# Batch 0's attention in plain float32, its probabilities turned on TensorE, and small work shared out anew over the engines

## The chip, the core and the metric

The kernel runs on one core of a Trainium2 chip. The metric is device time in microseconds (us) of one execution, as the median of three runs. The engines are TensorE (PE; PEld is its weight load), VectorE (DVE), ScalarE (ACT), GpSimd (POOL) and the DMA engines, whose transfers SyncE (SP) issues here.

## The reference

Block-causal attention (blocks of 64) is followed by a mixer over tokens and channels; 8 batches, 8 heads, 576 positions, head size 64, all in float32.

```python
scores = scale * np.matmul(q, k.transpose(0, 1, 3, 2))
scores = np.where(block_i >= block_j, scores, -1000000000.0)
attn = softmax(scores)
x = np.matmul(attn, v)                    # heads side by side: (8, 576, 512)
theta = x @ w_theta
y = einsum('ts,bsd->btd', w_tok_r, x * cos(theta)) + einsum('ts,bsd->btd', w_tok_i, x * sin(theta))
u = x + y
out = u + maximum(u @ w_ch, 0)
```

The weights w_theta, w_tok and w_ch arrive in float64, as pairs of 32-bit words.

## The kernel before

**Split products.** To keep float32's accuracy at the speed of narrow types, nearly every factor is split into a high and a low part, and a product is three matmuls: high x high, low x high, high x low. For q and k the parts are in a reduced-precision float32 type (F32R: `q_high`, `k_high` on POOL, L495 to L501; `q_low`, `k_low` on DVE, L503 to L510); for v, the probabilities, x, z and the weights in float16 (`v_first` on ACT, `v_second` on DVE, L515 to L520; `high` on ACT, `low` on DVE, L571 to L576). The profile prints F32R as f32 or fp32r.

**Attention.** A pair is two heads, whose scores lie in the upper and lower 64 rows of the array and run side by side. Per pair: loads of q, k and v; splits; `scores` "ab" (row blocks 3 and 2) and "c" (1 and 0) and `first_scores` "d"; nine `maxima` on DVE and nine `exponentials` on ACT, which write a head's probabilities `t`, 1664 columns wide; `high` and `low`, then `turn`, a DMA transpose of both parts from `p` to `pt` that SP issues (L578); `weighted` (L591, L596), the product with v, 42 matmuls of 65 columns for a head and 12 more for the second of a pair; `normalise` on DVE. Batch 0 has pairs 0 to 3.

**Mixer.** x is turned (batch 0 on TensorE, L650, from float32; later batches by DMA), split (`x_high`, `x_low`), multiplied by w_theta (`theta`, L680, 60 matmuls of 512 columns), turned into sines and cosines on ACT, whose function table changes between exponential and sine (L706, L563). `times_x` (L719, mostly POOL) multiplies them by x, `z_high` (ACT) and `z_low` (POOL or DVE) split them, `mix` (L743) multiplies by w_tok, `take_u` adds x, which `add_parts` and `unscale` (DVE, L751) prepared, `u_high` and `u_low` (POOL, L767; in the last batch DVE) split u, and `channel` (L775) multiplies by w_ch. In the first stage the 17 weight tiles also pass ACT and DVE (`exponent`, `narrow`, `most`, `high_part`, `low_part`); the largest size of a weight sets a power of two as its scale.

**Order.** Every step is a part with its needs. A number in the table TIMES for each part sorts them, and each engine's queue gets its instructions in that order and runs them strictly in it. BANKS says which of the eight PSUM banks a step takes. RUNNING inserts filler matmuls of ones at given places of the order (L955), whose result is not used; 111 in all.

Of the kernel before, what the change touches and what calls it, by code (L numbers as in the profile page):

```python
# [29 lines left out]
Z_POOL = (0, 1, 3)  # L30


TIMES = [
# [974 lines left out]
```

## Time and profile before

| what | value |
|---|---|
| time, median of 3 runs | 730.01 us (728.07 to 731.66) |
| profiled execution, its span | 725.2 us (no time beside the span is on its page) |
| mean granted TensorE clock | 0.971 |
| instructions | 18373 |
| HBM read, written | 43.06 MB, 9.44 MB |

The span runs from the first to the last instruction of one execution. The time of a run also has what lies around the span. Busy shares count an instruction's whole duration; matmuls overlap in the pipeline, so a busy TensorE says that something was under way. "Idle before, releaser" names what an engine waited for last.

### The profile page before, as it was taken

Reading aid. Unit: us, or ns where it says so; the run is one execution under the profiler, and the core shown is the slowest. Engines: PE = TensorE matmul, PEld = TensorE weight load, DVE = VectorE, ACT = ScalarE, POOL = GpSimd, SP = SyncE. Lnnn points to the kernel's source line nnn. Section 1 sums busy time; section 2 is a strip of 40 time slices with the busy share of each in tenths; the row PEclk is TensorE's granted clock in tenths of the full one; section 3 lists DMA queues with packets and bytes.
Section 4 is the critical chain, followed back from the end, with each engine's and each line's share of the span. In section 5 each row is a group of like instructions: output and inputs, shape, how many; then the busy total and the mean of one; then the engine's idle time right before and its main releaser. Section 6 shows DMA issues by size and latency. Waiting matters only on the chain.

```text
span 725.2 us, 18373 instructions
## 1 busy us (share of the span) xinstructions
PE 667.2 (92%) x7565; PEld 527.2 (73%) x7565; DVE 602.7 (83%) x1103; ACT 518.7 (72%) x813; POOL 295.1 (41%) x334
## 2 busy tenths in 40 slices
PE   8667497999979899999999999999999999999997
PEld 4455455789658776988688758877597868776777
DVE  5899998998988998899969977999889967963833
ACT  4978989665896869866986689866983879525410
POOL 3111128742283435833273525552273654342110
PEclk9768799999989999999999999999999999999999
DMA  8999944899979998679949948889967945570101
GB/s 290 256 257 238 266 101 102 172 184 188 238 137 168 175 204 179 156 166 203 209 132 171 183 114 155 203 164 195 208 125 163 189 96 113 109 127 5 66 1 66
DMA packets 272739, 117.38 MB, mean 162 GB/s; under 512 B 254096, under 2 KB 254096, under 8 KB 272656
## 3 DMA queue, kind: packets, MB, share of 16 engines
q1 hardware_dynamic: 272656, 116.22, 74.4%
q8 instruction: 59, 0.97, 0.6%
q14 instruction: 24, 0.20, 0.1%
HBM read 43.06 MB, written 9.44 MB: 72 GB/s over the span
## 4 chain that ended last, share of the span: by engine, by line
PE 48%; DVE 25%; DMA 12%; ACT 10%; issue 4%; POOL 0%; SPq 0%; DVEq 0%; ACTq 0%; POOLq 0%
PE ps L743 18%; PE ps L775 10%; PE ps L680 7%; PE ps L591 6%; DVE p L575 5%; DMA pt<-p 5%; PE ps L531 5%; DVE m L559 5%; ACT t L563 4%; DMA out<-u 2%; DVE v L519 2%; DVE zl L733 2%; DMA xt<-xp 1%; ACT p L572 1%; DMA raw_v<-in_v 1%
## 5 line engine op out<-in xcount | busy, mean ns | idle before, releaser
L563 ACT ACTIVATE t<-ps,m 128x576 f32<-128x576 f32 (+4 forms) x288 | 143.1, 556 | 65.4 <-DVE m L559 36.3
L743 PE MATMUL ps<-wT_h,zh 128*128 128x288 f16 x540 | 156.2, 289 | 9.6 <-ACT t L563 6.6
L743 PE MATMUL ps<-wT_h,zl 128*128 128x288 f16 x540 | 155.6, 288 | 0.6 <-DVE zl L733 0.4
L743 PE MATMUL ps<-wT_l,zh 128*128 128x288 f16 x540 | 155.6, 288 | 0.0
L559 DVE TENSOR_REDUCE m<-ps 128x1 f32<-128x448 f32 (+4 forms) x288 | 133.3, 508 | 11.1 <-PE ps L536 9.2
L575 DVE SCALAR_TENSOR_TENSOR p<-t,p 128x1664 f16<-128x1664 f32 x64 | 125.3, 1960 | 7.9 <-ACT p L572 7.8
L743 PEld LDWEIGHTS <-zh 128*128 128x128 f16 x1080 | 106.3, 98 | 28.5
L591 PE MATMUL ps<-v,pt 128*128 128x65 f16 x2688 | 95.9, 196 | 20.8 <-DVE xn L611 15.5
L572 ACT ACTIVATE p<-t 128x1664 f16<-128x1664 f32 x64 | 102.1, 1604 | 17.8 <-DMA pt<-p 17.6
L591 PEld LDWEIGHTS <-pt 128*128 128x128 f16 x2688 | 92.4, 99 | 28.0 <-DMA pt<-p 11.9
L680 PE MATMUL ps<-wth_h,xt 128*128 128x512 f16 x320 | 95.2, 379 | 2.6 <-DVE xt L668 0.9
L680 PEld LDWEIGHTS <-xt 128*128 128x128 f16 x480 | 46.3, 98 | 56.0 <-issue 3.4
L719 POOL TENSOR_TENSOR aa<-aa,xn 128x256 f32<-128x256 f32 (+1 forms) x84 | 64.3, 793 | 37.9 <-ACT aa L706 29.2
L775 PE MATMUL ps<-uh,wch_h 128*128 128x288 f32 x256 | 78.5, 307 | 0.4 <-DVE u L781 0.4
L531 PE MATMUL ps<-kh,qh 64*128 64x224 f32 (+3 forms) x384 | 66.3, 324 | 10.3 <-ACT t L563 9.2
L775 PE MATMUL ps<-ul,wch_h 128*128 128x288 f32 x256 | 75.5, 295 | 0.0
L775 PE MATMUL ps<-uh,wch_l 128*128 128x288 f32 x256 | 75.4, 295 | 0.0
L743 PEld LDWEIGHTS <-zl 128*128 128x128 f16 x540 | 53.3, 99 | 23.9 <-issue 10.8
L767 POOL TENSOR_TENSOR ul<-u,uh 128x576 fp32r<-128x576 f32 x28 | 44.1, 1576 | 63.3 <-ACT uh L761 63.1
L719 POOL TENSOR_TENSOR rr<-rr,xn 128x256 f32<-128x256 f32 x64 | 51.5, 829 | 40.9 <-ACT rr L707 35.4
L501 POOL TENSOR_SCALAR kh<-k 128x640 fp32r<-128x640 f32 x32 | 30.6, 957 | 73.8 <-DMA k<-in_kT 46.4
L680 PE MATMUL ps<-wth_l,xt 128*128 128x512 f16 x160 | 60.6, 379 | 0.0
(120 smaller groups left out, 1384.1 us busy)
## 6 DMA issues: line engine op xcount, KB each, us to landing
raw_v<-in_v SPq DMA_DIRECT2D x32, 384.0 KB, 4.2
q<-in_qT SPq DMA_DIRECT2D x32, 320.0 KB, 3.5
k<-in_kT SPq DMA_DIRECT2D x32, 320.0 KB, 3.5
out<-u SPq DMA_DIRECT2D x32, 288.0 KB, 2.6
w_raw<-in_w_tok SPq DMA_DIRECT2D x9, 576.0 KB, 5.5
...
pt<-p SPq DMA_TRANSPOSE x64, 6.4
```

Of the source, the lines that this page charges most:

```text
L501: nc.gpsimd.tensor_scalar(out=self.kh, in0=self.k, scalar1=1.0, scalar2=0.0, op0=ALU.mult, op1=ALU.add)
L531: nc.tensor.matmul(s[hh][:, col:col + n], lhsT=qq[rows, i * P:(i + 1) * P], rhs=kk[rows, k0:k0 + n], start=nn == 0 and (j == 0 or c == "ab ...
L559: nc.vector.tensor_reduce(out=m, in_=s, axis=AX.XY if i in (2, 3) else AX.X, op=ALU.max, negate=True)
L563: nc.scalar.activation(out=to, in_=s, func=AF.Exp, scale=1.0, bias=m)
L572: nc.scalar.mul(self.p[:, 0, :], self.t, LIFT)
L575: nc.vector.scalar_tensor_tensor(out=self.p[:, 1, :], in0=self.t, scalar=LIFT, in1=self.p[:, 0, :], op0=ALU.mult, op1=ALU.subtract)
L591: nc.tensor.matmul(o[:, i, :], lhsT=pp[:, block, :], rhs=vv[:, of, hh, :], start=nn == 0, stop=nn == n - 1)
L680: nc.tensor.matmul(g, lhsT=x[:, dt, part, i, :], rhs=ww[:, dt, :], start=(n == 0), stop=(n == 11))
L719: self.engine(n).tensor_tensor(out=cd, in0=cd, in1=self.rows(dt, i0, ni), op=ALU.mult)
L743: nc.tensor.matmul(g, lhsT=zz[:, kk, cols], rhs=ww[:, kk, ts], start=(n == 0 and kk == k0 and nn == 0), stop=(n == 4 and nn == 2))
L767: engine.tensor_tensor(out=ul[:, dt, ts], in0=self.u(dt)[:, ts], in1=uh[:, dt, ts].bitcast(F32), op=ALU.subtract)
L775: nc.tensor.matmul(g[:, 0:HS], lhsT=ww[:, dt, e * P:(e + 1) * P], rhs=uu[:, dt, th * HS:(th + 1) * HS], start=(n == 0), stop=(n == 11))
```

## The change

For batch 0 (pairs below `PLAIN`, 4) q, k, v and the probabilities stay whole in float32. Scores and the product with v are one float32 matmul where three stood: 13 for a pair's scores (39 before), 14 and 18 for its two heads' product with v (42 and 54). k is used as loaded, q and v get one scaling each. The probabilities are turned by 13 float32 transposes a head on TensorE into PSUM, in two halves of 8 and 5 blocks (`turn_half`, two banks each), and copied out with the factor LIFT by ACT or DVE (`keep_half`). So `high`, `low` and `turn`, and the remainders of q, k and v, are gone for these pairs. After them `count_keys` writes the columns of ones of v's tile anew for the later pairs.

A table ON names the engine (P, D or A) of single instructions: the splits `q_high` and `k_high`, the scaling of v, the copies, the products with x (`z`), the remainders `zl` and `ul`, and `unscale` (`xd`). Products with x on DVE go from 12 to 64 and on POOL from 148 to 96; `z_low` on DVE from 38 to 33; `u_low` on DVE from 8 to 18; 21 of 32 `unscale` go to ACT; of 60 splits of q and k that remain, with batch 0's four scalings of q, 28 are on ACT and 32 on POOL (64 on POOL before). Table loads of ACT go from 28 to 16, each time with one at the start. The whole order (PLACES in place of TIMES), the banks and the places of the fillers (56 in place of 111) are new.

```diff
...
-TIMES = [
-    100, 540, 615, 665, 745, 7122, 7220, 2640, 3104, 3223, 3533, 3619, 6960, 7153, 1595, 2055, 2169, 2280, 2497,
...
+PLACES = [
+    9, 39, 45, 50, 55, 274, 279, 7, 64, 66, 81, 86, 167, 174, 4, 20, 33, 37, 46, 150, 153, 12, 51, 57, 61, 62, 148,
...
-    (3, 0, 20), (33, 0, 26), (84, 0, 16), (137, 0, 8), (215, 0, 10), (265, 7, 10), (376, 0, 5), (442, 0, 12), (484,
-    0, 4)
+    (11, 0, 19), (35, 0, 10), (83, 0, 2), (96, 0, 5), (132, 5, 3), (443, 0, 8), (474, 3, 9)
 ]
+ON = {"qh": "APPPPPPPAAAAAAPPAPAAPAAPPAPAPAPA",
+      "vf": "DADP",
+      "cp": "DDADADAAADAAAAAA",
+      "kh": "DDDDPPPPAPPPPAAPAPPAAAPAPAAAPAPP",
+      "z": "DDDDPDDPPPPPPPPPDPPDPPPPPDDPPPDDPPDDDPDDPDPDPPPDDDPPPPPDPDPDPDPPPPPPDPDPPPPDDDPD",
+      "zl": "PPPDPPPPPDPPPPDPDPDPPPDDDPDPDPDDPDPPPPDDPPDDPDPPPPPDDDPPPPPDPPDPDDDPDDPDDDPPPDPD",
+      "xs": "DDDDDDDDDDDDDDDDDDDDDDDDDDDDDDDD",
+      "xd": "DAAADDAADADAAADAAAAAAAAADDDADAAD",
+      "ul": "PPPPPPPPDDPDPPPPDPDPDPDDPDPDDDDD"}
+PLAIN = 4
...
+    def engine_of(kind, n):
+
+        return {"P": nc.gpsimd, "D": nc.vector, "A": nc.scalar}[ON[kind][n]]
...
-            self.k = ld.tile([P, 640], F32, tag="kr", name="k")
+            self.k = ld.tile([P, 640], F32, tag="kr", name="k") if self.p >= PLAIN else \
+                ld.tile([P, 640], F32R, tag="kh", name="k", bufs=QK_BUFS).bitcast(F32)
             nc.sync.dma_start(out=self.k, in_=kT[self.b, self.pr])
+        def split(self, out, x, scale, engine):
+            if engine is nc.scalar:
+                engine.mul(out, x, scale)
+            else:
+                engine.tensor_scalar(out=out, in0=x, scalar1=scale, scalar2=0.0, op0=ALU.mult, op1=ALU.add)
...
-            nc.gpsimd.tensor_scalar(out=self.qh, in0=self.q, scalar1=QK_SCALE, scalar2=0.0, op0=ALU.mult, op1=ALU.add)
+            if self.p < PLAIN:
+                self.qh = self.qh.bitcast(F32)
+            self.split(self.qh, self.q, QK_SCALE, engine_of("qh", self.p))
...
-            nc.gpsimd.tensor_scalar(out=self.kh, in0=self.k, scalar1=1.0, scalar2=0.0, op0=ALU.mult, op1=ALU.add)
+            self.split(self.kh, self.k, 1.0, engine_of("kh", self.p))
...
+        def v_scaled(self):
+            x, engine = self.whole[:, :, :, 0:D], engine_of("vf", self.p)
+            if engine is nc.scalar:
+                engine.mul(x, self.v, self.batch.up)
+            else:
+                engine.tensor_scalar(out=x, in0=self.v, scalar1=self.batch.up, scalar2=1.0, op0=ALU.mult, op1=ALU.mult)
...
         def products(self):
+            if self.p < PLAIN:
+                return (self.qh, self.k),
             return (self.qh, self.kh), (self.ql, self.kh), (self.qh, self.kl)
...
+        def turn_half(self, half):
+            g = bank("tp", self.n, half)
+            for i in range((8, 5)[half]):
+                at_col = (8 * half + i) * P
+                nc.tensor.transpose(out=g[:, i * P:(i + 1) * P], in_=self.t[:, at_col:at_col + P], identity=ident)
+
+        def keep_half(self, half):
+            n = (8, 5)[half] * P
+            whole = self.turned.rearrange("p a c q -> p (a c q)").bitcast(F32)[:, 8 * half * P:8 * half * P + n]
+            engine, g = engine_of("cp", 2 * self.n + half), bank("tp", self.n, half)[:, 0:n]
+            if engine is nc.scalar:
+                engine.mul(whole, g, LIFT)
+            else:
+                engine.tensor_scalar(out=whole, in0=g, scalar1=LIFT, scalar2=None, op0=ALU.mult)
...
+            if pair.p < PLAIN:
+                products = [(self.turned.rearrange("p a c q -> p (a c q)").bitcast(F32).rearrange("p (c q) -> p c q", q=P), pair.whole)]
+            each = len(products)
...
-                self.engine(n).tensor_tensor(out=cd, in0=cd, in1=self.rows(dt, i0, ni), op=ALU.mult)
+                engine_of("z", (2 * self.b + hf) * 5 + n).tensor_tensor(out=cd, in0=cd, in1=self.rows(dt, i0, ni), op=ALU.mult)
...
-            engine = nc.gpsimd if n in Z_POOL and self.b < B - 1 else nc.vector
-            engine.tensor_tensor(out=zl, in0=cv, in1=zh, op=ALU.subtract)
+            engine_of("zl", (2 * self.b + hf) * 5 + n).tensor_tensor(out=zl, in0=cv, in1=zh, op=ALU.subtract)
...
-            nc.vector.tensor_scalar(out=self.u(dt), in0=self.u(dt), scalar1=self.batch.down, scalar2=None, op0=ALU.mult)
+            if engine_of("xd", self.b * NDT + dt) is nc.scalar:
+                nc.scalar.mul(self.u(dt), self.u(dt), self.batch.down)
+            else:
+                nc.vector.tensor_scalar(out=self.u(dt), in0=self.u(dt), scalar1=self.batch.down, scalar2=None, op0=ALU.mult)
...
-            engine = nc.vector if th else nc.gpsimd
-            engine.tensor_tensor(out=ul[:, dt, ts], in0=self.u(dt)[:, ts], in1=uh[:, dt, ts].bitcast(F32), op=ALU.subtract)
+            engine_of("ul", self.b * NDT + dt).tensor_tensor(out=ul[:, dt, ts], in0=self.u(dt)[:, ts], in1=uh[:, dt, ts].bitcast(F32), op=ALU.subtract)
...
+        split = [("ql", p), ("kl", p)] if p >= PLAIN else [("qh", p), ("k", p)]
+        add(("sab", p), step_of(pair.scores, "ab"), split, takes=[(("ab", p, hh), 2) for hh in range(2)])
...
+                free_pt = turn_of(f"pt{hh}", [("weighted", n)])
+                for half in range(2):
+                    needs = [key for key in made if (key[3] in (2, 3)) == (half == 0)]
+                    add(("tp", n, half), step_of(h.turn_half, half), needs, takes=[(("tp", n, half), 2)])
+                    add(("cp", n, half), step_of(h.keep_half, half), [("tp", n, half)] + free_pt, leaves=[("tp", n, half)])
+                turned_by = [("cp", n, half) for half in range(2)]
...
```

How the instructions move, at three places. The first is ACT's queue around the end of pair 0's exponentials; t_95 and t_96 before, t_91 and t_92 after are the two heads' probabilities. Before:

```order
L563 ACTIVATE t_95<-ps,m 128x192
L394 ACTIVATE w_val<-w_raw 128x512
L563 ACTIVATE t_96<-ps,m 128x192
L563 ACTIVATE t_96<-ps,m 128x448
L572 ACTIVATE p_100<-t_95 128x1664
L572 ACTIVATE p_101<-t_96 128x1664
L407 ACTIVATE wth_h,most_theta<-w_val 128x512
L407 ACTIVATE wT_h,most_tok<-w_val 128x576
```

and after the change:

```order
L571 ACTIVATE t_92<-ps,m 128x576
L571 ACTIVATE t_92<-ps,m 128x192
L396 ACTIVATE wth_h,most_theta<-w_val 128x512
L571 ACTIVATE t_92<-ps,m 128x448
L383 ACTIVATE w_val<-w_raw 128x512
L396 ACTIVATE wth_h,most_theta<-w_val 128x512
L590 ACTIVATE pt_99<-ps 128x1024
L396 ACTIVATE wth_h,most_theta<-w_val 128x512
```

The two whole-width high parts are gone; a copy of 1024 turned columns from PSUM stands between weight steps, and the copies of the first head's halves are on DVE.

The second is SP's queue in the first stage. Before:

```order
L513 DMA raw_v<-in_v 128x768
L385 DMA w_raw<-in_w_tok 128x1152
L385 DMA w_raw<-in_w_theta 128x1024
L579 DMA_TRANSPOSE pt_103<-p_101 128x26x128
L493 DMA k<-in_kT 128x640
L579 DMA_TRANSPOSE pt_102<-p_100 128x26x128
L385 DMA w_raw<-in_w_tok 128x1152 x2
L489 DMA q<-in_qT 128x640
L493 DMA k<-in_kT 128x640
L579 DMA_TRANSPOSE pt_102<-p_100 128x26x128
```

and after the change:

```order
L512 DMA raw_v<-in_v 128x768
L374 DMA w_raw<-in_w_theta 128x1024
L479 DMA q<-in_qT 128x640
L484 DMA k<-in_kT 128x640 x2
L374 DMA w_raw<-in_w_tok 128x1152 x2
L479 DMA q<-in_qT 128x640
L374 DMA w_raw<-in_w_tok 128x1152
L484 DMA k<-in_kT 128x640
L374 DMA w_raw<-in_w_tok 128x1152
L479 DMA q<-in_qT 128x640
L512 DMA raw_v<-in_v 128x768 x2
L374 DMA w_raw<-in_w_tok 128x1152 x2
```

The transposes from p to pt have left this stretch; only loads stand there, those of w_theta and v earlier.

The third is TensorE's queue around the first pair's product with v for its second head. Before (pt_103 holds the turned probabilities):

```order
L596 LDWEIGHTS pt_103
L596 MATMUL ps<-v_83,pt_103 64x65
L531 MATMUL ps<-kh,qh 128x288 x2
L531 MATMUL ps<-kh,ql 128x288 x2
L531 MATMUL ps<-kl,qh 128x288 x2
```

and after the change:

```order
L583 MATMUL ps<-ident_r,t_91 128x128 x5
L332 LDWEIGHTS ones
L332 MATMUL ps<-w_diag,ones 128x128
L617 MATMUL ps<-v_83,pt_99 128x65 x14
L622 MATMUL ps<-v_83,pt_99 64x65 x4
L539 MATMUL ps<-k,qh 128x288 x4
L539 MATMUL ps<-k,qh 128x224 x4
```

Where f16 products with a weight load each and sets of three score products stood, single float32 matmuls stand (18 for this head, 8 for the scores ab), and transposes of pair 1 (L583) are put ahead of the product.

## Rows read from the trace of the kernel before

**Rows 1.** The page, part 1: busy us, share of the span, instructions.

```profile
PE 667.2 (92%) x7565; PEld 527.2 (73%) x7565; DVE 602.7 (83%) x1103; ACT 518.7 (72%) x813; POOL 295.1 (41%) x334
```

**Rows 2.** The page, part 2: granted TensorE clock in 40 slices, tenths.

```profile
PEclk9768799999989999999999999999999999999999
```

**Rows 3.** Two stretches: length, busy us (instructions), granted clock, DMA share, GB/s.

```profile
0.00:97.20 97.20, 65.53 (x718) 47.76 (x719) 84.45 (x172) 76.43 (x138) 19.91 (x46) 0.82 0.92 245
97.20:726.00 628.80, 601.66 (x6847) 479.43 (x6846) 518.22 (x932) 442.23 (x676) 275.17 (x288) 0.99 0.72 149
```

**Rows 4.** Four shorter stretches, the same columns.

```profile
0.00:18.00 18.00, 15.21 (x89) 7.75 (x89) 10.06 (x18) 7.60 (x14) 5.69 (x27) 1.00 0.84 289
18.00:97.20 79.20, 50.31 (x630) 40.01 (x630) 74.40 (x155) 68.83 (x124) 14.22 (x19) 0.78 0.94 235
100.00:200.00 100.00, 93.90 (x1064) 71.96 (x1063) 90.43 (x155) 73.12 (x114) 47.60 (x45) 1.00 0.83 174
200.00:300.00 100.00, 92.22 (x1114) 72.83 (x1113) 87.97 (x157) 83.55 (x131) 52.81 (x61) 0.97 0.90 170
```

**Rows 5.** TensorE in order of time: start, us, what; matmuls' ends are modelled.

```profile
9.43 0.40 PE L531 MATMUL ps<-kh,qh 64*128 64x288 f32 x2
...
12.03 0.30 PE L543 MATMUL ps<-kh,qh 128*128 128x64 f32 x1
...
12.39 5.79 PE L955 MATMUL ps<-ones 128*128 128x512 bf16 x26
...
41.62 1.44 PE L591 MATMUL ps<-v,pt 128*128 128x65 f16 x42 [0.85 <-DMA pt<-p]
...
94.11 1.10 PE L650 MATMUL ps<-ident_r,xn 128*128 128x128 f32 x8
...
97.20 0.59 PE L680 MATMUL ps<-wth_h,xt 128*128 128x512 f16 x2 [0.92 <-DVE xt L668]
...
110.24 0.40 PE L531 MATMUL ps<-kh,qh 64*128 64x288 f32 x2
```

**Rows 6.** Groups by line, first 97.2 us: busy us, mean ns, idle before.

```profile
L575 DVE SCALAR_TENSOR_TENSOR p<-t,p 128x1664 f16<-128x1664 f32 x8 | 15.0, 1880 | 0.6 <-ACT p L572 0.6
L572 ACT ACTIVATE p<-t 128x1664 f16<-128x1664 f32 x8 | 12.7, 1606 | 1.2 <-DMA pt<-p 1.2
L563 ACT ACTIVATE t<-ps,m 128x576 f32<-128x576 f32 x10 | 7.5, 750 | 1.2 <-DVE m L559 1.1
L516 ACT ACTIVATE v<-raw_v,sizes 128x768 f16<-128x768 f32 x6 | 5.6, 957 | 1.3 <-PE ps L596 1.3
L519 DVE SCALAR_TENSOR_TENSOR v<-raw_v,sizes,v 128x768 f16<-128x768 f32 x5 | 5.1, 1011 | 0.0
L510 DVE TENSOR_TENSOR kl<-k,kh 128x640 fp32r<-128x640 f32 x6 | 4.9, 818 | 1.6 <-POOL kh L501 1.6
L505 DVE SCALAR_TENSOR_TENSOR ql<-q,qh 128x640 fp32r<-128x640 f32 x5 | 4.3, 857 | 3.8 <-POOL qh L497 3.8
```

**Rows 7.** DMA issues, first 97.2 us: median us from issue to landing.

```profile
pt<-p SPq DMA_TRANSPOSE x8, 7.1
```

**Rows 8.** Groups by line, whole run, as in rows 6.

```profile
L719 POOL TENSOR_TENSOR rr<-rr,xn 128x256 f32<-128x256 f32 x64 | 51.5, 829 | 40.9 <-ACT rr L707 35.4 <-DVE m L559 5.4
L751 DVE TENSOR_SCALAR u<-u,sizes 128x576 f32<-128x576 f32 x32 | 17.6, 561 | 0.0
L706 ACT ACT_TABLE_LOAD x14 | 18.0, 1283 | 0.2
L563 ACT ACT_TABLE_LOAD x13 | 16.7, 1283 | 1.2 <-DVE m L559 1.1
L719 DVE TENSOR_TENSOR aa<-aa,xn 128x256 f32<-128x256 f32 x8 | 2.9, 419 | 0.2 <-ACT aa L706 0.2
```

More of the change, by code (lines that the diff above doesn't have):

```diff
@@ L296, in attention_phase_mixer, with count_keys @@
     nc.gpsimd.memset(half_pi, math.pi / 2)
-    v_parts = [[const.tile([P, NV, 2, D + 1], F16, name=f"v{i}{j}") for j in range(2)] for i in range(2)]
-    for both in v_parts:
-        for part, x in zip(both, (1.0, 0.0)):
+    v_both = [const.tile([P, 2 * NV * 2 * (D + 1)], F16, name=f"v{i}") for i in range(2)]
+    v_parts = [[both.rearrange("p (a c h d) -> p a c h d", a=2, c=NV, h=2)[:, j] for j in range(2)] for both in v_both]
+    v_whole = [both.bitcast(F32).rearrange("p (c h d) -> p c h d", c=NV, h=2) for both in v_both]
+    def count_keys(*parts):
+        for part, x in zip(parts, (1.0, 0.0)):
             nc.gpsimd.memset(part[:, :, :, D:D + 1], x)
-    for both in v_parts:
-        nc.gpsimd.memset(both[0][0:64, 0, :, D:D + 1], 0.0)
-        nc.gpsimd.memset(both[0][64:P, 5, :, D:D + 1], 0.0)
+        nc.gpsimd.memset(parts[0][0:64, 0, :, D:D + 1], 0.0)
+        nc.gpsimd.memset(parts[0][64:P, 5, :, D:D + 1], 0.0)
+    for i in range(2):
+        count_keys(*([v_whole[i]] if i < PLAIN else v_parts[i]))
     t = [const.tile([P, WIDE], F32, name=f"t{i}") for i in range(2)]
@@ L484, in __init__ @@
             self.v1, self.v2 = v_parts[p % 2]
+            self.whole = v_whole[p % 2]
             self.v = raw_v[:, self.pr, :].rearrange("p (c h d) -> p c h d", c=NV, h=2)
@@ L531, in scores @@
                         nc.tensor.matmul(s[hh][:, col:col + n], lhsT=qq[rows, i * P:(i + 1) * P], rhs=kk[rows, k0:k0 + n],
-                                         start=nn == 0 and (j == 0 or c == "ab" and j == 1), stop=c == "ab" and j == 2 and nn == 2)
+                                         start=nn == 0 and (j == 0 or c == "ab" and j == 1), stop=c == "ab" and j == 2 and nn == len(self.products()) - 1)
             for hh in range(2):
@@ L542, in first_scores @@
             for nn, (qq, kk) in enumerate(self.products()):
-                nc.tensor.matmul(s[:, 0:64], lhsT=qq[:, 512:640], rhs=kk[:, 0:64], start=nn == 0, stop=nn == 2)
+                nc.tensor.matmul(s[:, 0:64], lhsT=qq[:, 512:640], rhs=kk[:, 0:64], start=nn == 0, stop=nn == len(self.products()) - 1)
         def where(self, hh, i):
@@ L596, in weighted @@
                             nc.tensor.matmul(o[rows, 4 + h, :], lhsT=pp[:, FIRST // P, h * 64:(h + 1) * 64], rhs=vv[:, 5, h, :],
-                                             start=nn == 0, stop=nn == 2)
+                                             start=nn == 0, stop=nn == each - 1)
         def normalise(self, step):
@@ L709, in attention_phase_mixer @@
         Z_PIECES = [(0, 0, 2, 0), (1, 0, 2, 4), (0, 2, 2, 2), (1, 2, 2, 6), (0, 4, 1, 8)]
-        def engine(self, n):
-            return nc.vector if self.b == B - 1 and n % 2 == 0 else nc.gpsimd
         def times_x(self, hf, n):
@@ L832, in attention_phase_mixer @@
             p = b * NPAIR + pr
-            add(("q", p), pairs[p].load_q, turn_of("qr", [("ql", p)]))
-            add(("k", p), pairs[p].load_k, turn_of("kr", [("kl", p)]))
-            add(("v", p), pairs[p].load_v, turn_of(f"raw_v{pr}", [("v2", p)]))
+            s_last = [("s" + c, p) for c in ("ab", "c", "d")]
+            add(("q", p), pairs[p].load_q, turn_of("qr", [("ql" if p >= PLAIN else "qh", p)]))
+            add(("k", p), pairs[p].load_k, turn_of("kr", [("kl", p)]) if p >= PLAIN else turn_of("kh", s_last, QK_BUFS))
+            add(("v", p), pairs[p].load_v, turn_of(f"raw_v{pr}", [("v2" if p >= PLAIN else "vf", p)]))
             add(("vz", p), step_of(batch.sum_of, pr), [("v", p)])
@@ L852, in attention_phase_mixer @@
         for c, first, second in (("q", pair.q_high, pair.q_low), ("k", pair.k_high, pair.k_low)):
-            add((c + "h", p), first, [(c, p)] + turn_of(c + "h", s_last, QK_BUFS))
-            add((c + "l", p), second, [(c + "h", p)] + turn_of(c + "l", s_last, QK_BUFS))
+            if p >= PLAIN or c == "q":
+                add((c + "h", p), first, [(c, p)] + turn_of(c + "h", s_last, QK_BUFS))
+            if p >= PLAIN:
+                add((c + "l", p), second, [(c + "h", p)] + turn_of(c + "l", s_last, QK_BUFS))
         free = turn_of(f"v{p % 2}", [("weighted", n) for n in heads])
-        add(("v1", p), pair.v_first, [("v", p), ("vc", b, 2)] + free)
-        add(("v2", p), pair.v_second, [("v1", p)])
-        add(("sab", p), step_of(pair.scores, "ab"), [("ql", p), ("kl", p)], takes=[(("ab", p, hh), 2) for hh in range(2)])
-        add(("sc", p), step_of(pair.scores, "c"), [("ql", p), ("kl", p)], takes=[(("c", p, hh), 1) for hh in range(2)])
-        add(("sd", p), pair.first_scores, [("ql", p), ("kl", p)], takes=[(("d", p), 1)])
+        if p < PLAIN:
+            add(("vf", p), pair.v_scaled, [("v", p), ("vc", b, 2)] + free)
+            if p >= PLAIN - 2:
+                add(("vo", p % 2), step_of(count_keys, *v_parts[p % 2]), turn_of(f"v{p % 2}", [("vo", p % 2)]))
+        else:
+            add(("v1", p), pair.v_first, [("v", p), ("vc", b, 2)] + free)
+            add(("v2", p), pair.v_second, [("v1", p)])
+        split = [("ql", p), ("kl", p)] if p >= PLAIN else [("qh", p), ("k", p)]
+        add(("sab", p), step_of(pair.scores, "ab"), split, takes=[(("ab", p, hh), 2) for hh in range(2)])
+        add(("sc", p), step_of(pair.scores, "c"), split, takes=[(("c", p, hh), 1) for hh in range(2)])
+        add(("sd", p), pair.first_scores, split, takes=[(("d", p), 1)])
         rows = [(hh, i) for i in (3, 2, 1, 0) for hh in range(2)] + [(1, 4)]
@@ L865, in attention_phase_mixer @@
             add(("m", p, hh, i), step_of(pair.maxima, hh, i), needs + (free if (hh, i) == (0, 3) else [("m", p, 0, 3)]))
-        free = [turn_of(f"t{hh}", [("low", n)]) for hh, n in enumerate(heads)]
+        free = [turn_of(f"t{hh}", [("low", n)] if p >= PLAIN else [("tp", n, half) for half in range(2)]) for hh, n in enumerate(heads)]
         for hh, i in rows:
@@ L876, in attention_phase_mixer @@
             h = Head(n, pair, hh, mixers[b])
-            add(("high", n), h.high, [("e", p, h_, i) for h_, i in rows if h_ == hh] + turn_of(f"p{hh}", [("turn", n)]))
-            add(("low", n), h.low, [("high", n)])
-            add(("turn", n), h.turn, [("low", n)] + turn_of(f"pt{hh}", [("weighted", n)]))
-            add(("weighted", n), h.weighted, [("turn", n), ("v2", p)] + turn_of("o", [("normalise", n, 2)]))
+            made = [("e", p, h_, i) for h_, i in rows if h_ == hh]
+            if p < PLAIN:
+                free_pt = turn_of(f"pt{hh}", [("weighted", n)])
[4 more added lines that the diff above has]
+                turned_by = [("cp", n, half) for half in range(2)]
+            else:
+                add(("high", n), h.high, made + turn_of(f"p{hh}", [("turn", n)]))
+                add(("low", n), h.low, [("high", n)])
+                add(("turn", n), h.turn, [("low", n)] + turn_of(f"pt{hh}", [("weighted", n)]))
+                turned_by = [("turn", n)]
+            add(("weighted", n), h.weighted, turned_by + [("v2" if p >= PLAIN else "vf", p)] + turn_of("o", [("normalise", n, 2)]))
             needs = [("weighted", n)] + turn_of("r", [("normalise", n, 2)], 2)
```

9 lines of the change are left out of this document (4 added, 5 removed), and 341 rows, old and new, of tables (BANKS, PLACES, TIMES).

## Prediction

> **What bounds the kernel now.** I read the shares of the engines first, then the same by stretches, then TensorE's instructions in order of time, and last the groups by line for prices.
>
> TensorE (PE) is busy for 667.2 of 725.2 us, VectorE (DVE) for 602.7, ScalarE (ACT) for 518.7 [rows 1]. That average hides two stages. The granted clock is below full speed in the first eighth of the span and nearly nowhere else [rows 2]. Batch 0's first product with w_theta is issued at 97.20 us [rows 5]; I call this T0 and cut there. Behind it lie 628.0 us of the span, with PE busy for 601.7 of them at a clock of 0.99 [rows 3]: the mixer and the other batches' attention are PE's. Ahead of it PE has 65.5 us of 97.2 at a clock of 0.82, and a good part of that is the filler products of L955. The reader should see who is full there: from 18 to 97.2 us DVE is busy for 74.4 of 79.2 us (94%), ACT for 68.8 (87%), and the DMA engines for 94% [rows 4]. So the first stage is DVE's, with ACT and the DMA close behind, and PE waits. The time is T0, plus 628.0, plus what lies around the span. The profiled span is 725.2 and the median of the three runs 730.0, so I add 4.8 at the end.
>
> **The change, stage one: DVE.** Batch 0 loses eight remainders of probabilities, 15.0 us ahead of T0. It also loses the remainders of q, k and v of its four pairs; some of batch 1's were already ahead of T0 and stay, so by the new order the count there falls by two of q (0.86 each), four of k (0.82) and three of v (1.01), 8.0 us [rows 6]. It gains five copies out of PSUM: one of 1024 columns, four of 640. No row has that operation; the nearest is ACT's exponential from PSUM, 0.75 us for 576 columns [rows 6], so 1024 columns lie between 0.75 and 1.33 (in proportion). I take 1.1, and 0.8 for 640, since nearly the same width is in the row: 4.3 us. Two scalings of v at about a v part's 0.95 add 1.9. DVE's 84.5 us ahead of T0 become 84.5 - 15.0 - 8.0 + 4.3 + 1.9 = 67.7.
>
> **ACT.** It loses eight high parts of probabilities (12.7 us) and four of v (3.7) [rows 6]. It gains eleven copies (seven of 1024 columns and four of 640: 10.9), one scaling of q (0.8) and one of v (0.9); by the new order one more high part, two more exponentials and one more sum stand ahead of T0 (3.5 together). 76.4 - 16.4 + 10.9 + 0.8 + 0.9 + 3.5 = 76.1 us: nothing gained. **ACT is the new bound of the stage.** It was idle for 10.4 of the first 18 us [rows 4]. The scores now need only k as it is loaded, second in SP's queue in place of fourth, and one scaling of q, no remainders; I give that 4 us, so 76 + 6 = 82 us if ACT never waits afterwards.
>
> **DMA.** Eight transposes leave SP's queue ahead of T0, each 7.1 us from issue to landing [rows 7]. What is left are the loads of weights, q, k and v, which kept pace at the start (289 GB/s in the first 18 us [rows 4]). I cost that stage's DMA at nothing: it lies beside ACT's 82 us.
>
> **PE, stage one.** Here stand the unknown prices.
> - Scores: a pair takes 2.96 us with three reduced-precision products (9.43 to 12.39) [rows 5]. The three leave out low times low; a whole float32 product could cost as little as one of them or as much as four. Between 0.99 and 3.95 a pair I take the upper end, 15.8 us for four pairs: with 192 to 320 moving columns nothing is left beside which a part could hide.
> - Transposes: 104. Eight float32 ones of L650 took 1.10 us [rows 5], 0.14 each: 14.3 us.
> - Products with v: 42 f16 products took 1.44 us, 0.034 each; the reduced-precision product with 64 moving columns, which also reads 32-bit weights, comes every 0.12 us [rows 5]. 112 full and 16 half products count as 120. The ends are one such product and, as above, four: 0.12 and 0.48. I take two, 0.24, nearer to the row: the stationary operand has two halves to load, and 65 moving columns, 0.034 us in f16, fit beside a load. 28.8 us; the ends are 14.4 and 57.6.
> - The rest: pair 4's scores 2.96, two thirds of pair 5's 2.0, 20 transposes of x 2.8, and 39 fillers at 13.04/60 = 0.22 each (the w_theta products have the same 512 columns [rows 5]) 8.5.
>
> Sum 15.8 + 14.3 + 28.8 + 16.3 = 75.2, from about 5 us on: 80. PE comes out just below ACT. Two in-order queues that feed each other at such loads don't run without waits: ACT's copy of a turned head stands in its queue behind the transposes, PE's next product behind the copy, the next pair's exponentials behind both. I add 6 us: **T0 = 88**. PE's waits should then be short, and its clock near full before T0.
>
> The trace shows no product of plain float32. The Trainium skill's page "FP8 and Floating Point Precision", section "TensorE Precision Notes", says that a true FP32 product takes four passes through the array. By that rule, with 0.12 us for a pass, an estimate for the products with v is 57.6 us in place of 28.8; that is the first rival below.
>
> **Stage two.** 628.0 us remain, less the 2.0 us of pair 5's scores done earlier. PE's list is otherwise the same, so the edits matter only where PE waits: 628.8 - 601.7 = 27 us [rows 3], of which 100 - 93.9 and 100 - 92.2 lie between 100 and 300 [rows 4]. The shared-out work: 52 more products with x on DVE (0.36 each against POOL's 0.83 [rows 8]), ten more remainders of u there (0.82, as k's [rows 6]), 21 scalings of u from DVE (0.56 [rows 8]) to ACT, 28 splits of q and k from POOL to ACT, and 27 table loads on ACT, 1.28 each [rows 8], become 15. DVE: 18.7 + 8.2 - 11.8 = +15, 518 to 533 of 628 us. ACT: 49 x 0.75 (576 columns [rows 6]) = 36.8, less 15.4, +21, 442 to 463. POOL gets less to do. I cost all of this at nothing: it lies beside PE's 96%; were that cover gone, DVE's 15 us or ACT's 21 would show, whichever queue PE then waited for. The relieved DVE should enter batch 1 with less backlog, and POOL's slow products leave the way from sines to mixing, so I take back 4 of the 14 us lost between 100 and 300; the bounds are 0 and 14.
>
> **Sum:** 88 + 628.0 - 2.0 - 4 + 4.8 = **714.8, say 715 us**.
>
> **Rivals.**
> 1. *Slower: the float32 products make PE the bound of stage one.* At 0.48 us each the sum of PE is 104 us, T0 = 109, nothing is taken back: 109 + 628.0 - 2.0 + 4.8 = 740. It decides from the price at which T0 exceeds 99 (99 + 630.8 = 730): 5 + 46.4 + 120w = 99, w = 0.40 us. For: no row has the operation, and the transposes and 64-column products suggest that loading 32-bit weights sets the pace. Against: the fillers that are left ahead of T0 stand at its beginning, so there is slack in PE there. Chance 0.20.
> 2. *Same: the removed load is not what T0 waits for.* ACT's 76 us stay; it now waits for PE's transposes where it waited for remainders, T0 stays near 97, and DVE's extra 15 us behind T0 eat what POOL's relief gives: 97 + 628.0 - 2.0 + 4.8 = 728. For: ACT's sum does not fall at all. Against: ACT had 20.8 us idle ahead of T0 [rows 3], and DVE was the fuller. Chance 0.13.
> 3. *More: both queues run dense and stage two loses nothing in batch 1.* T0 = 82, 14 us taken back: 82 + 628.0 - 2.0 - 14 + 4.8 = 699. For: the freed DVE and DMA. Against: PE's queue is in order and full as well. Chance 0.17.
>
> **The numbers.** My forecast (705 to 724) has 0.50, with rivals of 0.20, 0.13 and 0.17. About 0.5% is what a measurement of this kernel can tell from no change: 726.4 to 733.7. Faster 0.67, same 0.13, slower 0.20. For the range I leave out about half of rival 3 and half of rival 1: 700 to 738.
>
> **What would show it.** Right: the first w_theta product near 88 us; ahead of it DVE busy for about 68 us and ACT for about 76 with few idle stretches; a clock above 0.9 between 18 us and T0; the float32 products with v every 0.24 us; PE busy for 96% or more of the rest. Wrong: products with v at 0.40 us or more and ACT waiting for PE before its copies (rival 1); T0 near 97 with PE waiting for ACT (rival 2); or a stretch behind T0 in which PE waits for DVE's products with x, which would break the cost of nothing in stage two.

## The result and the profile after

The changed kernel takes 704.28 us (median of 4 runs, 702.33 to 706.13) where the kernel before takes 729.04 beside it (726.32 to 731.66): a ratio of 0.9664, 95% interval 0.9631 to 0.9696. The profiled execution took 702.33 us, with a span of 700.0.

First the page of the changed kernel, its shares and its clock (against [rows 1, 2]):

```profile
PE 671.2 (96%) x7434; PEld 538.9 (77%) x7434; DVE 598.7 (86%) x1126; ACT 532.6 (76%) x850; POOL 223.3 (32%) x252
...
PEclk9999999999999999999999999999999999999999
```

TensorE's clock no longer drops in the first eighth of the span. Then its first product with w_theta (T0) and, ahead of it, the float32 work of batch 0, in TensorE's order of time (start, duration):

```profile
9.64 2.00 PE L539 MATMUL ps<-k,qh 64*128 64x288 f32 x16
...
13.11 1.25 PE L998 MATMUL ps<-ones 128*128 128x512 bf16 x5
...
28.40 3.24 PE L617 MATMUL ps<-v,pt 128*128 128x65 f32 x28
31.47 1.04 PE L583 MATMUL ps<-ident_r,t 128*128 128x128 f32 x8
...
83.57 0.59 PE L706 MATMUL ps<-wth_h,xt 128*128 128x512 f16 x2 [0.65 <-DVE xt L694]
```

T0 is 83.57 us, against 97.20 [rows 5]. The span split there, and in stretches (busy us of PE, PEld, DVE, ACT, POOL, then clock, DMA share, GB/s), against [rows 3, 4]:

```profile
0.00:83.57 83.57, 73.46 (x612) 59.54 (x613) 68.67 (x162) 71.69 (x141) 21.29 (x49) 1.00 0.61 212
0.00:18.00 18.00, 14.26 (x73) 7.54 (x74) 6.47 (x14) 8.83 (x17) 2.70 (x21) 1.00 0.87 317
18.00:83.57 65.57, 59.20 (x540) 52.00 (x541) 62.20 (x149) 62.86 (x125) 18.59 (x28) 1.00 0.54 183
83.57:700.00 616.43, 597.74 (x6822) 479.37 (x6821) 530.04 (x965) 460.94 (x710) 202.06 (x203) 0.99 0.73 151
100.00:200.00 100.00, 92.85 (x1141) 74.98 (x1138) 92.56 (x172) 82.82 (x128) 39.17 (x41) 0.97 0.82 170
200.00:300.00 100.00, 97.92 (x1200) 79.97 (x1199) 92.45 (x162) 81.52 (x127) 36.65 (x38) 1.00 0.92 182
```

The span lost 25.2 us: 13.6 ahead of T0 and 11.6 behind it. From 18 us to T0 three engines are now full together (ACT 62.86 of 65.57 us, DVE 62.20, PE 59.20). Behind T0, DVE and ACT got busier by 11.8 and 18.7 us, and PE's time without work fell from 26.3 (628.0 - 601.7 [rows 3]) to 18.7; its busy time fell by the other 3.9.

### The profile page after: what moved, and what is told of

Same layout as the page of the kernel before. It is cut to its first block, busy times and chain, and to the rows that moved or that the text cites. A ratio compares the mean times of both kernels' runs of the same rounds, so it can differ in the third digit from the quotient of the medians.

```text
span 700.0 us, 18036 instructions
## 1 busy us (share of the span) xinstructions
PE 671.2 (96%) x7434; PEld 538.9 (77%) x7434; DVE 598.7 (86%) x1126; ACT 532.6 (76%) x850; POOL 223.3 (32%) x252
## 4 chain that ended last, share of the span: by engine, by line
PE 56%; ACT 16%; DVE 13%; DMA 9%; issue 3%; SPq 2%; POOL 0%; ACTq 0%; DVEq 0%; POOLq 0%
PE ps L765 24%; PE ps L799 9%; PE ps L617 7%; PE ps L539 6%; PE ps L706 6%; DMA pt<-p 3%; ACT t L571 3%; DVE m L567 3%; DMA raw_v<-in_v 3%; ACT p L595 2%; DMA q<-in_qT 1%; PE ps L998 1%; DMA xt<-xp 1%; ACT aa L732 1%; ACT aa L714 1%
## 5 line engine op out<-in xcount | busy, mean ns | idle before, releaser
L571 ACT ACTIVATE t<-ps,m 128x448 f32<-128x448 f32 (+4 forms) x288 | 143.9, 549 | 50.6 <-DVE m L567 34.6
L567 DVE TENSOR_REDUCE m<-ps 128x1 f32<-128x576 f32 (+4 forms) x288 | 134.7, 508 | 14.3 <-PE ps L544 14.0
L598 DVE SCALAR_TENSOR_TENSOR p<-t,p 128x1664 f16<-128x1664 f32 x56 | 106.4, 1902 | 9.7 <-ACT p L595 9.7
L617 PE MATMUL ps<-v,pt 128*128 128x65 f16 (+1 forms) x2576 | 108.2, 201 | 5.6 <-DMA pt<-p 2.2
L595 ACT ACTIVATE p<-t 128x1664 f16<-128x1664 f32 x56 | 88.7, 1590 | 8.9 <-DMA pt<-p 7.7
L617 PEld LDWEIGHTS <-pt 128*128 128x128 f16 x2352 | 78.5, 98 | 10.6 <-DMA pt<-p 4.8
L742 POOL TENSOR_TENSOR aa<-aa,xn 128x256 f32<-128x256 f32 (+1 forms) x60 | 45.8, 788 | 94.4 <-ACT aa L733 47.6
L765 PEld LDWEIGHTS <-zl 128*128 128x128 f16 x540 | 53.0, 98 | 18.7 <-POOL rr L742 4.1
L539 PE MATMUL ps<-kh,qh 64*128 64x288 f32 (+1 forms) x336 | 54.0, 313 | 1.5 <-ACT t L571 1.0
L799 PEld LDWEIGHTS ps<-uh,wch_h 128*128 128x128 f32 x256 | 48.1, 188 | 2.8 <-DVE rr L719 1.3
L539 PE MATMUL ps<-kh,ql 64*128 64x288 f32 (+1 forms) x336 | 48.9, 284 | 0.0
```

The costliest lines, as they stand in the source:

```text
L539: nc.tensor.matmul(s[hh][:, col:col + n], lhsT=qq[rows, i * P:(i + 1) * P], rhs=kk[rows, k0:k0 + n], start=nn == 0 and (j == 0 or c == "ab ...
L567: nc.vector.tensor_reduce(out=m, in_=s, axis=AX.XY if i in (2, 3) else AX.X, op=ALU.max, negate=True)
L571: nc.scalar.activation(out=to, in_=s, func=AF.Exp, scale=1.0, bias=m)
L595: nc.scalar.mul(self.p[:, 0, :], self.t, LIFT)
L598: nc.vector.scalar_tensor_tensor(out=self.p[:, 1, :], in0=self.t, scalar=LIFT, in1=self.p[:, 0, :], op0=ALU.mult, op1=ALU.subtract)
L617: nc.tensor.matmul(o[:, i, :], lhsT=pp[:, block, :], rhs=vv[:, of, hh, :], start=nn == 0, stop=nn == n - 1)
```

## The experiments

Twelve kernels ran, each timed in several rounds beside the kernel before; their ratios are to it, where the changed kernel has 0.9664. T0 (the "first channel product" of the expectations) and what follows it come from one profiled execution of each.

**1 to 3: one half of the change at a time.** They needed a rule that chooses banks, since the table of banks fits one order only; run 1 is the control for that rule.

```
e1: -at_bank = next(banks)
    +the banks that have been free longest; a step that finds none lets later steps go first
e2: e1, and PLACES, RUNNING, ON of the kernel before; turn_half and keep_half where "high" stood
e3: e1, and -PLAIN = 4
            +PLAIN = 0
    the splits of batch 0 beside the steps that had replaced them, its products with v one head later
```

> The changed kernel's steps in its own order and on its own engines, but every bank of PSUM chosen by a simple rule (the free bank that has been free longest) instead of the table of banks. It is the control for the two runs beside it, which need such a rule. My theory, that the banks themselves carry nothing: 702 to 708 us. Rival, that the chosen banks remove the waits of TensorE behind the first channel product: 708 to 716 us.

> Batch 0's attention in float32, transposed on TensorE, but the steps stand in the order of the kernel before and the engine table is the old one (banks by the rule of the control). Theory (float32 attention shortens stage one by freeing VectorE, the new order and sharing shorten the rest): the first channel product comes at 84 to 88 us instead of 97.2, what follows stays at 626 to 629 us, 712 to 718 us in all. Rival, the gain is the new order's alone: first channel product at 95 to 99 us, 725 to 730 us. Rival, the gain is float32's alone: 702 to 707 us.

> The new order and the new sharing over engines, but batch 0's attention in halves of float16 as before, its probabilities transposed by DMA. Theory: the first channel product at 95 to 98 us, what follows at 616 to 620 us, 712 to 718 us. Rival, the gain is the new order's alone: 702 to 707 us. Rival, float32's alone: 725 to 730 us.

Measured: e1 719.32 us, ratio 0.988 (0.9842 to 0.9917); e2 781.43, 1.0733; e3 768.67, 1.0569, with T0 at 86.12, 147.18 and 126.02 us. The control already missed: it loses 15 us. ScalarE, GpSimd and SyncE keep their orders in it, but on TensorE the scores of two pairs found no free bank and came later, at one place behind 24 mixing products and 42 products with v, at the other behind 12 and 54. One stretch shows the price, in e1 (columns as above):

```profile
150.00:170.00 20.00, 15.59 (x195) 13.63 (x192) 11.28 (x32) 8.57 (x15) 4.43 (x6) 0.74 0.65 132
```

and in the changed kernel:

```profile
150.00:170.00 20.00, 19.02 (x219) 17.88 (x216) 18.84 (x40) 14.78 (x23) 4.04 (x5) 1.00 0.82 167
```

In e1 TensorE, VectorE and ScalarE all have less to do there, and TensorE's granted clock is 0.74 in place of 1.00. In e2 and e3 the steps without a place in the table stood where I had put them, and both are far slower than either parent. So they don't say which half carries the gain; they say that neither half may be judged with steps put in by rule of thumb. The next runs leave an order as it is and change one thing in it.

**4 and 13: the sharing over engines.**

```
e4, changed kernel:
-ON = {"qh": "APPPPPPPAAAAAAPP...", "kh": "DDDDPPPPAPPP...", "z": "DDDDPDDPPPPPPPPP...", ...}
+ON = {"qh": "APPP" + "P" * 28, "kh": "P" * 32, "z": "P" * 70 + "DPDPD" * 2, "zl": "PPDPD" * 14 + "D" * 10,
+      "xd": "D" * 32, "ul": "P" * 28 + "D" * 4, ...}
e13, kernel before:
-self.engine(n).tensor_tensor(out=cd, ...)
+engine_of("z", (2 * self.b + hf) * 5 + n).tensor_tensor(out=cd, ...)
...
```

> The changed kernel with the old table of engines for the splits, the products with x and the sums (GpSimd carries the splits of w_channel's work and most z products again); order, banks and float32 attention as in the changed kernel. Theory, the order gives back the waits behind the first channel product and the sharing little of it: 704 to 708 us, first channel product at 83 to 85 us. Rival, the sharing carries them: 712 to 718 us, with TensorE waiting behind the first channel product for GpSimd.

> The kernel before, in its own order and with its own banks and attention, with the changed kernel's table of engines for the splits of q and k from batch 1 on, the products with x, the low halves of z and u, and the scaling of u. Theory after the run with the old table in the new order (table and order were made for each other): the first channel product stays at 96 to 98 us, what follows does not gain, 626 to 645 us, 724 to 742 us in all. Rival (the sharing alone took the waits behind the first channel product away): what follows 614 to 620 us, 712 to 718 us in all.

Measured: e4 747.22 us, 1.0269 (1.0232 to 1.0307); e13 742.81, 1.0193 (1.0149 to 1.0236). The two stretches on either side of T0, in e4:

```profile
0.00:85.14 85.14, 73.31 (x613) 59.52 (x614) 68.67 (x162) 71.74 (x141) 20.87 (x49) 1.00 0.61 208
85.14:745.50 660.36, 609.46 (x6822) 484.45 (x6821) 523.38 (x929) 432.62 (x662) 262.45 (x287) 0.98 0.69 141
```

and in e13:

```profile
0.00:97.33 97.33, 66.03 (x718) 47.68 (x719) 84.82 (x172) 76.43 (x139) 20.02 (x46) 0.82 0.96 245
97.33:736.90 639.57, 605.20 (x6847) 480.61 (x6846) 527.16 (x968) 472.44 (x724) 199.26 (x204) 0.99 0.71 146
```

Ahead of T0 the sharing does little. Behind it: old order with old sharing 628.0 us [rows 3], old order with new sharing 639.6, new order with old sharing 660.4, new with new 616.4. ("Order" includes the banks, the fillers and batch 0's attention here, which e4 and e13 don't part; e13's profiled execution is 3.8 us below its median.) Each alone is a loss, both together a gain of 11.6. In e4 TensorE's mixing products wait 12.6 us for ScalarE's exponentials in place of 5.8, and its busy time is 11.7 us longer. TensorE's longest waits behind T0 (us in total, times, longest) in e4:

```profile
PE ps L765 <- ACT t L571: 12.6, 7, 6.2
PE ps L539 <- DVE u L805: 6.3, 1, 6.3
PE ps L617 <- DVE xn L637: 6.1, 6, 2.2
```

and in the changed kernel:

```profile
PE ps L765 <- ACT t L571: 5.8, 4, 4.0
PE ps L617 <- DMA pt<-p: 2.2, 5, 0.7
PE ps L617 <- DVE xn L637: 1.8, 1, 1.8
```

My expectation of e4 was wrong by some 40 us, its rival by some 30, and the longest waits are for ScalarE and VectorE, not for GpSimd; that of e13 held on both sides of T0, though the whole is 0.8 us above its 742.

**5 to 7: more work for one engine ahead of T0** (idempotent, nothing else moves).

```
e5, in exponentials (e6: in maxima, around tensor_reduce):
+for _ in range(2 if self.p < PLAIN and i in (2, 3) else 1):
     nc.scalar.activation(out=to, in_=s, func=AF.Exp, scale=1.0, bias=m)
e7, in turn_half:
-for i in range((8, 5)[half]):
+for i in list(range((8, 5)[half])) * 2:
```

> The changed kernel with the exponentials of the two widest row groups of batch 0 issued twice (the second writes the same values again): some 10.6 us more for ScalarE ahead of the first channel product, nothing more for VectorE and TensorE. Theory (ScalarE bounds stage one, 62.9 of 65.6 us busy from 18 us on): that product comes 8 to 11 us later, at 92 to 94 us, 711 to 715 us. Rival, VectorE bounds it: at most 3 us later, 704 to 707 us.

> The changed kernel with the maxima of the two widest row groups of batch 0 taken twice: some 11 us more for VectorE ahead of the first channel product, nothing more for the others. Theory (ScalarE bounds, VectorE follows closely at 62.2 of 65.6 us): 4 to 8 us later, 708 to 712 us. Rival, VectorE is the bound: the full 10 to 11 us, 714 to 716 us. Rival, TensorE is the bound: at most 3 us.

> The changed kernel with each of batch 0's 104 transposes on TensorE issued twice, into the same place: some 14 us more for TensorE ahead of the first channel product. Theory (TensorE is 59.2 of 65.6 us busy and not the bound): the first 6 us are hidden, the rest shows, 6 to 9 us later, 710 to 714 us. Rival, TensorE bounds stage one: 13 to 15 us later, 717 to 719 us. Rival, it has slack by other waits: 0 to 2 us.

Measured: e5 723.66 us, 0.9919 (0.9884 to 0.9953); e6 726.15, 0.9955 (0.9927 to 0.9982); e7 706.35, 0.97 (0.9667 to 0.9733). The stretch from 18 us to T0 (columns as above) in e5:

```profile
18.00:99.42 81.42, 67.34 (x542) 59.26 (x541) 63.97 (x150) 73.95 (x142) 17.76 (x28) 0.90 0.44 148
```

in e6:

```profile
18.00:103.69 85.69, 72.54 (x541) 65.36 (x541) 74.00 (x163) 65.45 (x127) 17.69 (x28) 0.82 0.42 141
```

and in e7:

```profile
18.00:89.73 71.73, 67.81 (x632) 61.87 (x632) 63.34 (x150) 63.17 (x125) 18.44 (x28) 1.00 0.50 168
```

Ahead of T0 ScalarE got 11.1 us more in e5, and T0 came 15.9 later; VectorE 12.8 more in e6, T0 20.1 later. Both are paid more than once over, beyond what either theory expected; and ScalarE does not bound the stage alone, as I had it: VectorE does as much. Where they slow it, TensorE pauses, its clock is granted at 0.90 and 0.82, and what it does then takes longer. 28 records of products with v, a head's full ones, take 3.24 to 3.34 us in the changed kernel (above); in e5 one head of eight takes 6.08, in a stretch with a granted clock of 0.50 (1.2 of 2.4 GHz), after 7 us in which TensorE was busy for 3.6. In TensorE's order of time:

```profile
57.05 6.08 PE L618 MATMUL ps<-v,pt 128*128 128x65 f32 x28
```

More work for TensorE itself (e7) keeps the clock at 1.00, and T0 comes only 6.2 us later for 104 more transposes (14.2 us), as the theory had it. The whole kernel does not show even that: its 706.35 us miss the theory's 710 to 714, and the intervals of e7 and the changed kernel overlap.

**8, 11, 12: the DMA transposes and VectorE's remainders.**

```
e8, changed kernel, in keep_half, and a fill of p_parts[0] with 0 at the start:
+if half: nc.sync.dma_start_transpose(out=p_parts[1] ..., in_=p_parts[0] ...)
e11, kernel before, in turn, and a fill of p_turned with 1.0 at the start:
+if self.n >= 8:
     nc.sync.dma_start_transpose(out=self.turned ..., in_=self.p ...)
e12, kernel before, in low, and a fill of the low halves with 0 at the start:
+if self.n >= 8:
     nc.vector.scalar_tensor_tensor(out=self.p[:, 1, :], ...)
```

> The changed kernel with the eight removed DMA transposes of batch 0's probabilities put back beside the ones on TensorE, at the times of the new copies, out of a buffer of zeros into one that batch 0 doesn't read: the DMA traffic of before in stage one, without VectorE's and ScalarE's halves. Theory (VectorE's relief shortened stage one, the DMA transposes cost nothing there): 703 to 706 us, first channel product at 83 to 85 us. Rival, it was the DMA transposes that delayed the loads of stage one: 708 to 717 us, with the exponentials or scores waiting for DMA.

> The kernel before with the eight DMA transposes of batch 0's probabilities left out (its products with v read a buffer of ones): all splits, and so VectorE's and ScalarE's work, stay. Theory (VectorE, 77 of 82 us busy, bounds stage one of the kernel before; the transposes are hidden): first channel product at 94 to 98 us, 725 to 729 us. Rival (the transposes, and SP's queue that waits with them, delayed stage one, as the run with transposes added to the changed kernel would have it): first channel product at 83 to 88 us, 712 to 718 us.

> The kernel before with batch 0's eight low halves of the probabilities on VectorE left out (zeros stand in their place): 15.0 us less for VectorE [rows 6], all else stays, the DMA transposes and the order too. Theory (VectorE is the bound): first channel product 9 to 15 us sooner, at 82 to 88 us, 713 to 720 us. Rival (DMA): 0 to 4 us sooner, 724 to 729 us.

Measured: e8 722.85 us, 0.9929 (0.9904 to 0.9954); e11 730.91, 1.0037 (1.0017 to 1.0058); e12 726.53, 0.9979 (0.9955 to 1.0004). The stretch ahead of T0 in e12:

```profile
0.00:97.92 97.92, 66.03 (x718) 48.64 (x719) 72.40 (x166) 76.26 (x139) 17.82 (x46) 0.83 0.96 243
```

and in e11:

```profile
0.00:100.85 100.85, 69.30 (x719) 50.88 (x719) 90.76 (x174) 76.09 (x139) 21.19 (x46) 0.80 0.47 169
```

e12 is the main finding. VectorE has 12.1 us less to do than before [rows 3] (15.0 of remainders, less 1.5 of new fills and 1.4 by which the rest of its list is longer), and T0 does not move (97.92 against 97.20): my theory expected 9 to 15 us. The DMA share stays high, 0.96 (0.92 before). e11 takes the transposes away, the DMA share falls from 0.92 to 0.47, and T0 is 3.7 us later. Two fills of 2.8 us each that I had put on VectorE's queue stand in front there: its first maxima start at 15.84 us, against 12.83 before. So without them T0 would probably stay about where it was; no run shows that. Neither load alone is what T0 waits for. The chain of waits that ended last in the run, as shares by line of its part up to T0, tells why. The kernel before:

```profile
by line: DVE m L559 12.3%; DVE p L575 10.3%; DMA pt<-p 8.7%; issue 7.1%; DVE wT_l L418 6.7%; ACT t L563 5.3%; DMA w_raw<-in_w_theta 5.3%; PE ps L591 4.9%; DMA k<-in_kT 4.7%; DVE w_val L403 3.7%; DVE wth_l L418 3.2%; DMA q<-in_qT 3.1%; DVE w
```

e12, without the remainders:

```profile
by line: DMA pt<-p 8.4%; DVE m L561 8.2%; DMA w_raw<-in_w_ch 8.0%; ACT t L565 7.6%; DMA w_raw<-in_w_theta 6.6%; issue 6.3%; SPq L582 5.4%; DVE w_val L405 4.3%; DVE wT_l L420 3.8%; ACT p L574 3.3%; ACT w_val L396 3.3%; DMA q<-in_qT 3.2%; DMA
```

e11, without the transposes:

```profile
by line: DVE m L561 12.1%; issue 11.3%; DVE p L577 9.0%; DVE wT_l L420 6.5%; DVE w_val L405 6.2%; ACT t L565 5.8%; PE ps L533 4.7%; DVE v L521 4.6%; DMA w_raw<-in_w_theta 4.5%; DVE w_val L403 3.9%; DVE wth_l L420 3.7%; DVE pt L313 3.2%; ACT
```

and the changed kernel:

```profile
by line: DVE m L567 14.1%; ACT t L571 8.4%; PE ps L998 8.4%; DVE w_val L392 7.9%; issue 7.6%; DVE w_val L390 6.2%; ACT unused L445 5.3%; DVE wT_l L407 5.2%; ACT wT_h L401 3.5%; ACT wT_h L396 3.3%; ACT w_val L383 3.0%; ACT pt L590 2.9%; DVE 
```

All pieces of that chain up to T0, added up by engine, in us (in the changed kernel it passes T0 on ScalarE):

| kernel | VectorE | DMA and SyncE's queue | ScalarE | TensorE |
|---|---|---|---|---|
| before | 47.6 | 21.7 | 9.8 | 8.9 |
| e12, without the remainders | 25.8 | 37.2 | 22.2 | 5.1 |
| e11, without the transposes | 61.0 | 4.5 | 14.1 | 9.4 |
| changed | 40.8 | 0 | 25.4 | 9.2 |

Two ways to T0 are about equally long. One is VectorE's: maxima, remainders (DVE p), weights. The other is the DMA queue's: transposes, and loads that stand behind them in SyncE's queue. There a transpose (L582 in e12) waits for its probabilities, 9.9 us in two times:

```profile
SPq L582 <- ACT t L565: 9.9, 2, 6.9
```

The longer wait ends at 33.7 us; from 34.88 on the next transpose holds the queue for another 4.83 us, without a wait that the profile shows, and behind it goes the load of w_tok that the chain takes at 40.43. (The w_theta load on these chains is ahead of the first transpose, and the w_ch load of e12 stands behind one of v.) Without the remainders the second way remains, without the transposes the first. The change removes both at once: no DMA is left on its chain. TensorE's part hardly differs, so its higher clock ahead of T0 (1.00 for 0.82) is by this chain not what brought T0 forward.

In e8 the transposes come back, and T0 is 100.18 us, with the other engines' lists as they were but for a fill of 1.4 us on VectorE. The chain up to it, by line:

```profile
by line: SPq L591 10.9%; DMA w_raw<-in_w_tok 10.5%; DMA p<-p 8.2%; DVE m L568 7.9%; PE ps L1002 7.5%; PE ps L621 5.9%; issue 5.1%; ACT t L572 4.7%; DMA raw_v<-in_v 4.2%; PE ps L584 4.2%; DVE wT_l L408 3.9%; ACT w_val L384 2.7%; DVE xt L698 
```

It shows SyncE's queue held up at the transposes (L591) and, right behind them, loads of w_tok (issued at 29.3 us) and of v (at 71.5). The size is too large, since my spare transposes share one target, and each waits for the one ahead (11.4 us of SyncE's time), where the kernel before has two. So e8, which came out beyond both expectations, shows the path and not its price.

**9: the start.** The first scores wait for 19 fillers, 7.02 us, though q is scaled at 4.6.

```
- (11, 0, 19)
+ (11, 0, 7)
```

> The changed kernel with 7 instead of 19 fillers ahead of the first scores. Theory (the fillers, and not the split of q, set the start of the first scores at 9.6 us): the first scores start at 5 to 6 us, the first channel product 1 to 4 us sooner, 700 to 704 us. Rival (without them the first scores run at the half clock and give it back): first channel product at 83 to 90 us with a granted clock under 0.95 in the first 18 us, 704 to 712 us.

Measured: 703.6 us (702.91 to 704.11), ratio 0.9664 (0.963 to 0.9698). TensorE's start in order of time:

```profile
2.69 3.17 PE L998 MATMUL ps<-ones 128*128 128x512 bf16 x7 [2.69 <-POOL v L286]
5.79 2.42 PE L539 MATMUL ps<-k,qh 64*128 64x288 f32 x16
```

and the two stretches:

```profile
0.00:81.13 81.13, 70.25 (x601) 58.00 (x602) 69.25 (x162) 71.59 (x141) 20.60 (x49) 1.00 0.63 219
81.13:701.70 620.57, 600.45 (x6822) 480.72 (x6821) 529.81 (x965) 461.24 (x710) 200.03 (x203) 0.99 0.73 150
```

The scores start 3.9 us earlier, T0 comes 2.4 us earlier, and the rest takes 4.1 us more: nothing is won in all. Between fillers and T0 now stand loads of w_tok (14.5% of the chain in its stretch up to T0). The clock is 1.00 ahead of T0, so the rival's half clock did not come. None of the runs beats the changed kernel by more than its interval.

## Why the prediction was right, and where not

By its own sum it said 88 + 628.0 - 2.0 - 4 + 4.8 = 714.8; the profiled execution has 83.57 + 616.43 + 2.3 = 702.3. The direction held, and the stated range of 700 to 738, and both stages gained. But 704.28 us lie just below the 705 to 724 that had the chance of 0.50, and nearer to rival 3 (T0 at 82, 699 us in all) than to the forecast.

- **T0, 88 forecast, 83.57 measured.** VectorE's load ahead of it was 67.7 in the sum and is 68.67. ScalarE's was 76.1 and is 71.69: the copies took 10.2 us, not 10.9, and the next pairs' exponentials that I counted ahead of T0 partly come behind it. Its idle time, my 6 + 6 us, is 83.57 - 71.69 = 11.9. So the term that was mis-sized is ScalarE's list, by 4.4 us. That the idle time came out is luck: the 4 us that I gave for an earlier start did not come (first scores at 9.64, before 9.43 [rows 5]), ScalarE idles for 9.2 us in the first 18 where I had 6, and for 2.7 behind them where I had 6.
- **The reason for T0 was only half of it.** "The first stage is DVE's, with ACT and the DMA close behind" took the fullest engine for the bound, and the DMA was costed at nothing. By e12 VectorE's 12 us alone are worth nothing, by e11 the transposes alone neither. The sum came out since the change takes both ways away. That both removed in the old order would give the 13.6 us was not tried. Rival 2, "the removed load is not what T0 waits for", is what each part does by itself.
- **ScalarE as the new bound** fell too: e5 and e6 show that work added to it and to VectorE comes through alike, and with a surplus. The three engines are coupled, and TensorE's clock is part of it: the chain up to T0 has 39.4 us of TensorE in e5 and 38.7 in e6, against 9.2.
- **The prices of float32 on TensorE were right**, in the groups by line ahead of T0 (busy us, mean ns):

```profile
L617 PE MATMUL ps<-v,pt 128*128 128x65 f32 x224 | 26.4, 275 | 0.9 <-DVE sizes L448 0.5 <-DVE xn L637 0.3
...
L583 PE MATMUL ps<-ident_r,t 128*128 128x128 f32 x104 | 14.2, 278 | 3.4 <-ACT t L571 1.4 <-DVE pt L592 1.4 <-ACT pt L590 0.5
...
L590 ACT ACTIVATE pt<-ps 128x1024 f32<-128x1024 f32 x7 | 7.3, 1040 | 0.0
...
L592 DVE TENSOR_SCALAR pt<-ps 128x640 f32<-128x640 f32 x4 | 3.3, 818 | 0.0
L590 ACT ACTIVATE pt<-ps 128x640 f32<-128x640 f32 x4 | 2.9, 735 | 0.0
```

  A product with v leaves two records; 14 products from 28.40 to 31.47 us are 0.22 each (0.24 taken), the transposes 14.2 us (14.3), a pair's scores 13.11 - 9.64 = 3.47 (3.95), the copies 1.04 and 0.74 to 0.82 (1.1 and 0.8). Rival 1 needed 0.40 a product. The Trainium skill's page "FP8 and Floating Point Precision", section "TensorE Precision Notes", with its four passes gives an estimate of 0.48 at 0.12 for a pass: for these short products the trace does not bear that estimate out. For the wider scores it is nearer: 3.47 us a pair, against 4 x 0.99 = 3.95.
- **Stage two, 6 us forecast, 11.6 measured.** I took back 4 us of TensorE's waits and got 7.6 (of 26.3, not of my 27, whose stretch ends 0.8 us behind the span); its busy time there fell by 3.9 us, not by pair 5's 2.0 alone. From 200 to 300 us PE's busy time went from 92.2 [rows 4] to 97.9; from 100 to 200 it did not rise, so the place was half right. "I cost all of this at nothing" fails as a statement on the sharing: in the old order the same sharing costs 11.6 us (e13), and the new order without it 44 (e4). ScalarE's load behind T0 came to 461 (463 forecast). VectorE's came to 530 (533), and that is luck: the 52 products moved to it took 32.6 us where I had 18.7 (last section), the ten remainders 7.5 and the scalings gave back 10.2, but the rest of its list there got 18.1 us shorter, which I had at nothing. The same 28 instructions on xp (L668, now L694) take 23.4 us in place of 28.0, with the new sharing alone 25.5 (e13), with the new order alone 25.6 (e4); why is open.
- **Around the span** I added 4.8 us, the median less the profiled span; the changed kernel's runs have 2.3 (702.33 - 700.0), so the term was 2.5 us too large. Of the 4.8 only 1.8 lie around the span in the later runs of the kernel before (731.66 - 729.9); the other 3.0 are the difference between executions, which did not belong there.

Open: what each of order and banks does behind T0, since e1 moved scores as well; and why what follows T0 takes some 4 us more in e5, e6, e8 and e9 (620.6 to 622.0) than in the changed kernel (616.4) and e7 (615.9), though the order behind is the same.
